# A fused attention and channel-mix kernel: weights in a layout by groups, one store per tile, the last tile in halves, and a searched order

## The chip, the cores and the metric

The kernel runs on one core of a Trainium2 chip. The metric is the time of one execution on the device in microseconds (us); less is better. Engine names are those of the profile: PE is TensorE, DVE is VectorE, ACT is ScalarE, POOL is GpSimd, SP is SyncE, which issues the stores. Labels such as L691 are line numbers of the kernel; the same line can have another number in another run's kernel.

## The reference, cut to what matters

```python
q_s = softmax(q, axis=-1); k_s = softmax(k, axis=2)          # 8 batches, 8 heads, 576 x 64
x = q_s @ (k_s^T @ v)                                        # -> 8 x 576 x 512
xk = mu_k * x + (1 - mu_k) * x_prev                          # x_prev: the token before
xr = mu_r * x + (1 - mu_r) * x_prev
out = sigmoid(xr @ w_r) * (relu(xk @ w_k) ** 2 @ w_v)        # w_k 512x1024, w_v 1024x512, w_r 512x512
```

The output is 4608 rows of 512 float32, 9.44 MB.

## The kernel before

The kernel describes its operations with guessed durations, a small list scheduler in it puts them in an order, and each engine's instructions are emitted in that order. Each batch makes its attention in two groups of four heads (`g` = 0, 1). Each group fills two of the four channel tiles of `xk` and `xr`. The channel mix then works on units of 512 tokens.

Group `g` owns the channel tiles `g` and `g + 2`, and wk comes in one load per group:

```python
    def emit_wk(g):
        ap = bass.AP(tensor=moe_w_k.tensor, offset=moe_w_k.offset + g * 128 * F,
                     ap=[[F, 128], [256 * F, 2], [1, F]])
        ld = nc.gpsimd.dma_start(out=wk_bf[:, g::2, :], in_=ap)
    ...                                             # (cut)
            for cts in ((0, 2), (1, 3)) if early else (range(CT),):
                # matmuls of group 0's two tiles first, then group 1's (cut)
                nc.tensor.matmul(bank(kf)[:, 0:n], lhsT=wk_bf[:, ct, fc::FT],
                                 rhs=xs[0][:, ct, c0:c0 + n], ...)
```

A tile of the output is 128 tokens. They are two pieces of 64 rows in memory, because a column holds position `64 j + r` for row `r * 9 + j`: the rows of one piece are 9 rows apart. It is stored with one DMA for each piece:

```python
            def gated(...):   # DVE: ot = (tanh + 1) * v, 128 x 512
            def store(ot=ot, c=c, half=half):
                for i in range(2):
                    jb = (RING * half + c) // 64 + i
                    bb, j = jb // J, jb % J
                    dst = bass.AP(tensor=out.tensor, offset=out.offset + (bb * S + j) * C,
                                  ap=[[J * C, 64], [1, C]])
                    nc.sync.dma_start(out=dst, in_=ots[ot.index][64 * i:64 * i + 64, :])
```

There are three `ot` buffers in turn, so the fourth tile's gate cannot write before the first tile's store has landed.

The softmax here doesn't subtract the row's maximum and nothing guards it: scores larger than these inputs give would overflow.

## Time and profile before

| | before |
|---|---|
| time, median of 3 runs (range) | 206.43 us (205.68 to 206.51) |
| span of the profiled run | 203.8 us |
| granted PE clock | 1.00 |
| first L691 matmul; second | 16.72 us; 19.17 us |
| last gate starts; span ends | 199.24 us; 203.8 us |
| DMAs of the stores | 72 of 128 KB |

Three lines of the page of before: the span; the busy time of each engine with its share of the span and its instructions; and a count of the DMA packets. A packet under 512 bytes is too short for the data of a store (a row is 2 KB).

```profile
span 203.8 us, 5315 instructions
...
PE 187.2 (92%) x2163; PEld 103.0 (51%) x2163; DVE 162.7 (80%) x348; ACT 135.0 (66%) x211; POOL 39.6 (19%) x63
...
DMA packets 15040, 40.72 MB, mean 200 GB/s; under 512 B 2204, under 2 KB 2728, under 8 KB 15016
```

The windows view of before: in each stretch, its length, then the busy time and count of each engine, the granted clock, the DMA share and GB/s.

```profile
17.40:19.15 1.75, 0.00 (x0) 0.00 (x0) 0.00 (x0) 0.00 (x0) 0.31 (x1) 1.00 1.05 388
...
40.00:60.00 20.00, 19.54 (x343) 10.75 (x341) 19.70 (x36) 19.65 (x29) 8.10 (x12) 1.00 1.04 400
...
120.00:140.00 20.00, 20.00 (x244) 11.16 (x243) 19.24 (x41) 15.65 (x23) 0.00 (x0) 1.00 0.24 55
```

PE is full from 20 us on, except for short waits between 40 and 70 us. But in the first of these stretches, 1.75 us long, no engine computes (POOL's 0.31 us are a load being issued), while the DMA engines run at 388 GB/s. The timeline says what is awaited (the bracket gives the idle time before an instruction and what ended it):

```profile
16.72 0.65 PE L691 MATMUL mm_c<-xk,wk_bf 128*128 128x512 bf16 x1 [0.44 <-DMA wk_bf<-in_moe_w_k_dram]
...
19.17 0.65 PE L691 MATMUL mm_c<-xk,wk_bf 128*128 128x512 bf16 x1 [1.80 <-DMA wk_bf<-in_moe_w_k_dram]
```

The first matmul waits for the first wk load, as it must. The second reads channel tile 2 of the same load, yet waits 1.80 us more, for the second load. Its tile lies between tiles 1 and 3 of that load, whose interleaved pattern covers it: a false overlap.

The tail, from the timeline (x2 counts instructions in the row):

```profile
197.26 1.89 PE L732 MATMUL mm_b<-wv_bf,k_b 128*128 128x512 bf16 x8
...
198.23 1.11 SPq L748 DMA_DIRECT2D out_dram<-ot_b  x2
199.24 0.69 DVE L738 SCALAR_TENSOR_TENSOR ot_c<-th_b,mm_b 128x512 f32<-128x512 f32 x1 [1.04 <-PE mm_b L732]
199.96 1.11 SPq L748 DMA_DIRECT2D out_dram<-ot_c  x2
```

From the start of the last gate to the end of the span there are 203.8 - 199.24 = 4.56 us.

### The profile page before, as it was taken

How to read it: one execution, taken by the hardware profiler on the slowest of the kernel's cores; microseconds unless marked ns; L12 is line 12 of the kernel's file. 1: busy time of each engine (PE TensorE's matmuls, PEld its weight loads, DVE VectorE, ACT ScalarE, POOL GpSimd, SP SyncE). 2: the span in 40 equal slices, each digit the busy share in tenths (PEclk: the TensorE clock that was granted, in tenths of full speed). 3: DMA queues.
4: the chain of work that ended last, by engine and by line, in shares of the span. 5: the costliest groups of instructions: out<-in, count | busy, mean ns of one | idle time of the engine just before them, and what ended most of it. 6: DMA issues, size and time to landing. Idle time of an engine off the chain costs nothing.

```text
span 203.8 us, 5315 instructions
## 1 busy us (share of the span) xinstructions
PE 187.2 (92%) x2163; PEld 103.0 (51%) x2163; DVE 162.7 (80%) x348; ACT 135.0 (66%) x211; POOL 39.6 (19%) x63
## 2 busy tenths in 40 slices
PE   2455999999999999999999999999999999999990
PEld 0241554455644564565467565556556544654840
DVE  2793575799998999999999999999999759832531
ACT  5571696699999896957449788947663643552430
POOL 1682527544353421411100000000000000000000
PEclk9999999999999999999999999999999999999999
DMA  6999999999999999994582220332025122403504
GB/s 211 378 227 329 251 256 401 388 401 406 391 405 393 411 400 398 343 337 171 154 233 53 55 53 3 69 90 51 3 63 119 28 51 55 103 0 69 121 20 103
DMA packets 15040, 40.72 MB, mean 200 GB/s; under 512 B 2204, under 2 KB 2728, under 8 KB 15016
## 3 DMA queue, kind: packets, MB, share of 16 engines
q0 software_dynamic: 7504, 27.40, 39.5%
q1 hardware_dynamic: 7224, 12.40, 21.6%
q10 hardware_dynamic: 288, 0.59, 0.9%
q8 instruction: 17, 0.28, 0.6%
q14 instruction: 7, 0.06, 0.1%
HBM read 33.56 MB, written 9.44 MB: 211 GB/s over the span
## 4 chain that ended last, share of the span: by engine, by line
PE 72%; DVE 10%; DMA 8%; ACT 5%; issue 2%; POOL 0%; SPq 0%; DVEq 0%; ACTq 0%
PE mm_b L691 8%; PE mm_a L732 8%; PE mm_c L691 7%; PE mm_d L691 7%; PE mm_c L732 6%; PE mm_a L691 6%; PE mm_d L732 6%; PE mm_b L732 6%; PE mm_d L722 4%; DMA wk_bf<-in_moe_w_k_dram 4%; PE mm_c L722 4%; DMA raw_d<-in_q_dram 3%; PE mm_a L722 3%; PE mm_b L722 2%; PE att_b L497 2%
## 5 line engine op out<-in xcount | busy, mean ns | idle before, releaser
L691 PEld LDWEIGHTS <-wk_bf 128*128 128x128 bf16 x320 | 43.1, 145 | 24.2 <-DMA wk_bf<-in_moe_w_k_dram 3.2
L691 PE MATMUL mm_b<-xk,wk_bf 128*128 128x512 bf16 (+1 forms) x100 | 24.1, 357 | 0.5 <-DVE xk L553 0.3
L722 PEld LDWEIGHTS <-xr 128*128 128x128 bf16 x144 | 14.0, 98 | 16.3 <-issue 0.2
L732 PEld LDWEIGHTS <-k_b 128*128 128x128 bf16 x144 | 13.7, 98 | 15.8 <-issue 0.2
L732 PEld LDWEIGHTS <-k_a 128*128 128x128 bf16 x144 | 13.5, 98 | 15.3
L691 PE MATMUL mm_d<-xk,wk_bf 128*128 128x512 bf16 (+1 forms) x80 | 20.8, 372 | 0.0
L691 PE MATMUL mm_c<-xk,wk_bf 128*128 128x512 bf16 (+1 forms) x72 | 17.9, 364 | 2.2 <-DMA wk_bf<-in_moe_w_k_dram 2.2
L691 PE MATMUL mm_a<-xk,wk_bf 128*128 128x512 bf16 (+1 forms) x68 | 17.4, 369 | 0.0
L732 PE MATMUL mm_a<-wv_bf,k_a 128*128 128x512 bf16 x48 | 12.3, 380 | 0.0
L732 PE MATMUL mm_c<-wv_bf,k_b 128*128 128x512 bf16 x48 | 12.3, 379 | 0.0
L722 PE MATMUL mm_d<-wr_bf,xr 128*128 128x512 bf16 x44 | 11.3, 379 | 0.0
L732 PE MATMUL mm_d<-wv_bf,k_b 128*128 128x512 bf16 x40 | 10.3, 379 | 0.0
L732 PE MATMUL mm_b<-wv_bf,k_a 128*128 128x512 bf16 x40 | 10.3, 379 | 0.0
L722 PE MATMUL mm_c<-wr_bf,xr 128*128 128x512 bf16 x40 | 10.3, 379 | 0.0
L722 PE MATMUL mm_a<-wr_bf,xr 128*128 128x512 bf16 x36 | 9.3, 379 | 0.0
L676 ACT ACTIVATE rel_c<-mm_b 128x512 bf16<-128x512 f32 (+1 forms) x11 | 6.3, 574 | 4.1 <-PE mm_b L691 4.0
L732 PE MATMUL mm_a<-wv_bf,k_b 128*128 128x512 bf16 x32 | 8.2, 379 | 0.0
L732 PE MATMUL mm_d<-wv_bf,k_a 128*128 128x512 bf16 x32 | 8.2, 379 | 0.0
L727 ACT ACTIVATE th_b<-mm_c 128x512 f32<-128x512 f32 x7 | 4.2, 596 | 5.7 <-PE mm_c L722 4.9
L676 ACT ACTIVATE rel_a<-mm_b 128x512 bf16<-128x512 f32 (+1 forms) x9 | 4.8, 532 | 4.1 <-PE mm_b L691 3.8
L680 DVE TENSOR_TENSOR k_b<-rel_a 128x512 bf16<-128x512 bf16 (+1 forms) x14 | 5.5, 394 | 1.9 <-ACT rel_a L676 1.4
L484 PE MATMUL att_a<-ident,qs_a 64*64 64x64 bf16 x288 | 4.3, 201 | 2.6 <-DVE qs_a L452 2.6
(272 smaller groups left out, 419.6 us busy)
## 6 DMA issues: line engine op xcount, KB each, us to landing
out_dram<-ot_a SPq DMA_DIRECT2D x24, 128.0 KB, 3.0
out_dram<-ot_b SPq DMA_DIRECT2D x24, 128.0 KB, 4.2
out_dram<-ot_c SPq DMA_DIRECT2D x24, 128.0 KB, 2.4
raw_c<-in_v_dram POOLq DMA_DIRECT2D x3, 576.0 KB, 7.7
raw_a<-in_q_dram POOLq DMA_DIRECT2D x2, 576.0 KB, 10.4
raw_b<-in_k_dram POOLq DMA_DIRECT2D x2, 576.0 KB, 9.9
raw_d<-in_q_dram POOLq DMA_DIRECT2D x2, 576.0 KB, 11.1
raw_e<-in_k_dram POOLq DMA_DIRECT2D x2, 576.0 KB, 11.4
```

The source lines that it names most:

```text
L484: nc.tensor.transpose(out=transposed()[64 * u:64 * u + 64, hf, 64 * j:64 * j + 64], in_=qss[qs.index][r, j, 64 * u:64 * u + 64], identity= ...
L497: nc.tensor.matmul(bank(xp)[64 * hf:64 * hf + 64, u, at + c:at + e], lhsT=w[r, hf, :], rhs=qts[qt.index][r, hf, src:src + e - c], start=(n ...
L676: nc.scalar.activation(out=rels[rel.index][:, 0:n], in_=bank(kf)[:, 0:n], func=ACT.Relu, scale=HALF_ROOT)
L680: nc.vector.tensor_tensor(out=k2s[k2.index][:, fc, 0:n], in0=rels[rel.index][:, 0:n], in1=rels[rel.index][:, 0:n], op=ALU.mult)
L691: nc.tensor.matmul(bank(kf)[:, 0:n], lhsT=wk_bf[:, ct, fc::FT], rhs=xs[0][:, ct, c0:c0 + n], start=(ct == 0), stop=(ct == CT - 1))
L722: nc.tensor.matmul(bank(rps), lhsT=xs[1][:, ct, c:c + 128], rhs=wr_bf[:, ct, :], start=(ct == 0), stop=(ct == CT - 1))
L727: nc.scalar.activation(out=ths[th.index][:], in_=bank(rps), func=ACT.Tanh, scale=0.5)
L732: nc.tensor.matmul(bank(vps), lhsT=k2s[k2.index][:, ft, 128 * m:128 * m + 128], rhs=wv_bf[:, ft, :], start=(ft == 0), stop=(ft == FT - 1))
```

## The change

Four intentions: no false overlap on wk; a shorter tail; a better order, found by search; and fewer store issues. The diff, cut to its core (the scheduler's own code was also made faster and got new guesses; that is cut):

```diff
-LOOK = {"PE": 0.03, "ACT": 0.1, "DVE": 0.3, ...}
-AHEAD = (1.0, 4, 2)
+LOOK = {"PE": 0.017, "ACT": 0.686, "DVE": 0.274, ...}
+EARLY = (-0.88, 2.53, 7.27, ...)                 # a lead for each batch and group
+LOADS = ("wk0", "q10b", "wk1", "v10a", "q10a", "wr", "k10a", "wv0", ...)
-WIDE = "DVE"
+WIDE = "ACT"
...
-        ld = nc.gpsimd.dma_start(out=wk_bf[:, g::2, :], in_=ap)
+        ld = nc.gpsimd.dma_start(out=wk_bf[:, 2 * g:2 * g + 2, :], in_=ap)
...                       (xk and xr in the same layout; wr's rows indexed to match)
-            for cts in ((0, 2), (1, 3)) if early else (range(CT),):
+            for cts in ((0, 1), (2, 3)) if early else (range(CT),):
...
+            parts = 2 if half == B // 4 - 1 and c + 128 == RING else 1
+            w = C // parts
...                       (v matmuls, gate and store for each of the parts, e = 0, w, ...)
-            def store(ot=ot, c=c, half=half):
+            def store(e, ot=ot, c=c, half=half, w=w):
+                at = []
                 for i in range(2):
                     jb = (RING * half + c) // 64 + i
-                    bb, j = jb // J, jb % J
-                    dst = bass.AP(tensor=out.tensor, offset=out.offset + (bb * S + j) * C,
-                                  ap=[[J * C, 64], [1, C]])
-                    nc.sync.dma_start(out=dst, in_=ots[ot.index][64 * i:64 * i + 64, :])
+                    at.append((jb // J * S + jb % J) * C)
+                dst = bass.AP(tensor=out.tensor, offset=out.offset + at[0] + e,
+                              ap=[[at[1] - at[0], 2], [J * C, 64], [1, w]])
+                nc.sync.dma_start(out=dst, in_=ots[ot.index][:, e:e + w])
```

So every tile, not only the last, is now stored by one DMA.

## The prediction

> **What bounds it now.** TensorE. In the windows view it is busy without a break from 20.0 to 199.2 us of a 203.8 us span, at clock 1.00. Warm 128x512 matmuls stand 0.216 us apart (groups of four: 0.86 us in the chain of waits). Counted at that step, the matmuls from 20 to 199 us are some 173 us of work in 179 us. The rest is a cold start ([...]pairs take 1.0 us at 20.4 and 22.1 us, 0.43 us from 23.7 us), switches to and from small attention matmuls, and about 1 us of real waiting at 45 to 69 us, where DVE is 96 to 98% busy. So time can be won at the ends: before 20 us and after 199 us.
>
> **Head.** wk comes in two loads. The first L691 matmul starts at 16.72 us, when the first half lands. The second needs channel tile 2, also of the first half, but in the interleaved layout it is ordered behind the second half and starts at 19.17 us; wk_bf's DMA is its releaser in the waits (1.8 us idle). TensorE runs in order, so the attention matmuls of group 1 wait behind it; ACT waits 6.0 us and DVE 3.3 us for them. With contiguous groups, 8 matmuls over the first half (3.4 us cold) and attention pieces fill 17.15 to 19.17 us: 2.0 us. The new order puts 288 KB of q before the second wk half (0.7 us later, about 19.9 us); the filling work lasts past that. The warm-up comes earlier too.
>
> **Tail.** After the last matmul (199.16 us): gate 0.69 us, two store issues of about 0.56 us in a row, transfer; DMA activity ends about 202.5 us, the span at 203.8 us. In halves the last gate is about 0.42 us, one issue goes away, and half the bytes remain while the first half's store ran under the matmuls: 0.9 us. The matmuls keep their sum (128x256 groups of four step 0.44 us). Elsewhere merged stores save SP time that nobody waits for.
>
> **Order.** Total bytes before the last v of batch 1 are the same, so that lands near 37 us as before, and TensorE comes there 2 us earlier. Up to 0.5 us may be lost to this and to DVE, nearly full from 40 to 160 us. Retimed leads, other joins of attention blocks and the mu copy moved from DVE to ACT may give 0.3 to 1.5 us of waits and switches back. Net: 0.4 us gain.
>
> **Sum.** 2.0 + 0.9 + 0.4 = 3.3 us: span 200.5 us, time 206.4 - 3.3 = 203.1 us. Eight in ten: 201.4 to 204.8 us. Chances: faster by over 2% (under 202.3 us) 0.30, within 2% 0.69, slower 0.01.
>
> **What would show it.** Right: the second L691 matmul follows the first at about 17.1 us with no DMA wait; unit 0's last L691 ends near 28.4 us instead of 30.4; the last matmul ends near 196.7 to 197.2 us; from there to the end of the span takes 3.7 us instead of 4.6. Wrong: a wait for the second half of wk after the first eight matmuls, or new waits for xk or DVE between 38 and 50 us.
>
> **What would make it wrong.** Batch 1 too late for a TensorE that is 2 us earlier, so the head gain turns into a wait there (time about 205); or the search finding more than I credit, removing most switches and DVE waits between 36 and 70 us (about 201.5).

## The result, and the profile after

| | before | after |
|---|---|---|
| time, median (range) | 206.47 us (205.68 to 206.53), 4 runs | 277.6 us (276.96 to 279.3), 4 runs |
| span of the profiled run | 203.8 us | 277.5 us |
| mean granted clock | 1.00 | 0.888 |

The ratio is 1.347, with a 95% interval of 1.340 to 1.354. A ratio is the mean time of one kernel's fast runs over that of the other's of the same rounds, so it is not quite the ratio of the medians quoted. The kernel is 71 us slower; the prediction was 3.3 us faster.

The same lines of the page, after, with the line that gives the chain of waits by engine:

```profile
span 277.5 us, 5271 instructions
...
PE 202.1 (73%) x2171; PEld 107.7 (39%) x2171; DVE 161.7 (58%) x348; ACT 137.5 (50%) x212; POOL 40.4 (15%) x65
...
DMA packets 14138, 40.72 MB, mean 147 GB/s; under 512 B 1174, under 2 KB 1954, under 8 KB 14114
...
DMA 58%; PE 21%; DVE 13%; issue 1%; DVEq 0%; SPq 0%; ACT 0%; ACTq 0%
DMA out_dram<-ot_b 23%; DMA out_dram<-ot_c 21%; DMA out_dram<-ot_a 8%; PE mm_c L714 3%; DMA wk_bf<-in_moe_w_k_dram 3%; PE mm_d L714 3%; PE mm_b L714 3%; PE mm_a L714 2%; DMA raw_d<-in_q_dram 2%; PE mm_b L757 2%; DVE ot_c L763 2%; PE mm_c L747 1%; DVE qs_b L468 1%; DVE ot_b L763 1%; DMA raw_a<-in_q_dram 1%
```

DVE, ACT and POOL have the work they had (within 3 us). PE's busy time grew by 15 us, and its granted clock fell to 0.888 in the mean. The traces show the two together: just before a wait of 5.7 us, a group of four 128x512 matmuls takes 0.87 us (from 89.76 us to the next group at 90.63 us); just after it, at 97 to 101 us, the granted clock is 0.50 and a group of four takes 1.7 us. The chain is no longer PE but stores: 52% of the span is spent on three names, `out_dram<-ot_a`, `ot_b` and `ot_c`. PE is at 73%. The waits view of DVE, after, shows how the stores get hold of the compute engines (engine and line, what was waited for, us in total, times, longest):

```profile
DVE ot_b L763 <- DMA out_dram<-ot_b: 21.8, 5, 10.1
DVE ot_c L763 <- DMA out_dram<-ot_c: 20.7, 5, 7.4
DVE ot_a L763 <- DMA out_dram<-ot_a: 19.8, 5, 7.7
```

In before, no wait for a store is among DVE's nine longest; the longest is 3.3 us, for PE. After, gates wait 62 us for the `ot` buffers to come free. DVE's instructions are emitted in one order, and while a gate waits DVE is idle (that is the time in the bracket below), so the squares and the attention behind it wait too. PE then runs out of operands and of `mm` banks (the buffers that its matmuls write). Here an L714 matmul waited 5.70 us for the gate of `ot_b`:

```profile
97.35 1.87 PE L714 MATMUL mm_b<-xk,wk_bf 128*128 128x512 bf16 x4 [5.70 <-DVE ot_b L763]
```

The timeline of DVE shows one of its waits, and the chain puts the store behind it at 32 us:

```profile
73.19 0.69 DVE L763 SCALAR_TENSOR_TENSOR ot_b<-th_a,mm_c 128x512 f32<-128x512 f32 x1 [10.12 <-DMA out_dram<-ot_b]
```

```profile
40.74 32.32 DMA out_dram<-ot_b
```

The number that gives the cause away is in the DMA view of 225 to 260 us, after the loads are done (queue, kind: packets, MB, share of 16 engines):

```profile
DMA packets 889, 1.82 MB, mean 52 GB/s; under 512 B 12, under 2 KB 12, under 8 KB 887
...
q1 hardware_dynamic: 887, 1.79, 13.1%
```

The stores move 52 GB/s without a pause, at 13.1% of 16 engines. Two engines of 16 are 12.5% (the shares of this view run a little high: 1.04 in before, with all 16 busy). In before, stores come in bursts of up to 217 GB/s, in slices of 1 us, with gaps between.

The head did improve in this trace too: the first pair of L714 matmuls runs without a break (two from 17.76 us in 1.07 us, in the chain). That gain is drowned.

### The profile page after: what moved, and what is told of

Same layout as the page of the kernel before. It is cut to its first block, busy times and chain, and to the rows that moved or that the text cites. A ratio compares the mean times of both kernels' runs of the same rounds, so it can differ in the third digit from the quotient of the medians.

```text
span 277.5 us, 5271 instructions
## 1 busy us (share of the span) xinstructions
PE 202.1 (73%) x2171; PEld 107.7 (39%) x2171; DVE 161.7 (58%) x348; ACT 137.5 (50%) x212; POOL 40.4 (15%) x65
## 2 busy tenths in 40 slices
DMA packets 14138, 40.72 MB, mean 147 GB/s; under 512 B 1174, under 2 KB 1954, under 8 KB 14114
## 3 DMA queue, kind: packets, MB, share of 16 engines
HBM read 33.56 MB, written 9.44 MB: 155 GB/s over the span
## 4 chain that ended last, share of the span: by engine, by line
DMA 58%; PE 21%; DVE 13%; issue 1%; DVEq 0%; SPq 0%; ACT 0%; ACTq 0%
DMA out_dram<-ot_b 23%; DMA out_dram<-ot_c 21%; DMA out_dram<-ot_a 8%; PE mm_c L714 3%; DMA wk_bf<-in_moe_w_k_dram 3%; PE mm_d L714 3%; PE mm_b L714 3%; PE mm_a L714 2%; DMA raw_d<-in_q_dram 2%; PE mm_b L757 2%; DVE ot_c L763 2%; PE mm_c L747 1%; DVE qs_b L468 1%; DVE ot_b L763 1%; DMA raw_a<-in_q_dram 1%
## 5 line engine op out<-in xcount | busy, mean ns | idle before, releaser
L714 PEld LDWEIGHTS <-wk_bf 128*128 128x128 bf16 x320 | 45.9, 148 | 60.8 <-issue 42.4
L714 PE MATMUL mm_c<-xk,wk_bf 128*128 128x512 bf16 (+1 forms) x84 | 23.8, 402 | 17.4 <-DVE ot_a L763 7.9
L714 PE MATMUL mm_b<-xk,wk_bf 128*128 128x512 bf16 (+1 forms) x76 | 21.7, 406 | 13.7 <-DVE ot_b L763 8.1
L714 PE MATMUL mm_d<-xk,wk_bf 128*128 128x512 bf16 (+1 forms) x96 | 26.4, 394 | 0.9 <-DVE ot_a L763 0.9
L714 PE MATMUL mm_a<-xk,wk_bf 128*128 128x512 bf16 (+1 forms) x64 | 17.3, 395 | 0.5 <-DVE ot_c L763 0.5
L757 PE MATMUL mm_b<-wv_bf,k_b 128*128 128x512 bf16 (+1 forms) x56 | 13.5, 364 | 1.7 <-DVE ot_c L763 1.7
L699 ACT ACTIVATE rel_c<-mm_c 128x512 bf16<-128x512 f32 (+1 forms) x8 | 4.6, 572 | 15.0 <-PE mm_c L714 8.7
L757 PE MATMUL mm_c<-wv_bf,k_a 128*128 128x512 bf16 x40 | 10.3, 380 | 0.0
L699 ACT ACTIVATE rel_a<-mm_d 128x512 bf16<-128x512 f32 (+1 forms) x9 | 5.2, 576 | 9.5 <-DVE k_b L703 8.4
L699 ACT ACTIVATE rel_b<-mm_b 128x512 bf16<-128x512 f32 (+1 forms) x8 | 4.4, 545 | 9.3 <-PE mm_b L714 8.6
L699 ACT ACTIVATE rel_b<-mm_c 128x512 bf16<-128x512 f32 (+1 forms) x7 | 4.0, 567 | 9.7 <-DVE k_a L703 5.1
L757 PE MATMUL mm_a<-wv_bf,k_a 128*128 128x512 bf16 x32 | 8.3, 380 | 0.0
## 6 DMA issues: line engine op xcount, KB each, us to landing
raw_d<-in_q_dram POOLq DMA_DIRECT2D x2, 576.0 KB, 12.5
```

Of the source, the lines that this page charges most:

```text
L699: nc.scalar.activation(out=rels[rel.index][:, 0:n], in_=bank(kf)[:, 0:n], func=ACT.Relu, scale=HALF_ROOT)
L757: nc.tensor.matmul(bank(vps)[:, 0:w], lhsT=k2s[k2.index][:, ft, 128 * m:128 * m + 128], rhs=wv_bf[:, ft, e:e + w], start=(ft == 0), stop=( ...
```

## The experiments

### First question: is it the stores, the order, or the form of the DMA?

Theory 1: the one store of a tile runs on 2 of 16 DMA engines (after has 13.1% of 16 in the view above) because its target's slowest dimension has size 2; then the divisors of that size matter, which the cuts into 62 + 2, 48 + 16 and 57 + 7 rows below test. Theory 2: the searched order makes the waits. Theory 3: one large DMA with three dimensions is slow by its size or form.

**after_two_stores**: the changed kernel, with the stores given back as two.

```diff
+                for i in range(2):
+                    jb = (RING * half + c) // 64 + i
+                    at = (jb // J * S + jb % J) * C
+                    dst = bass.AP(tensor=out.tensor, offset=out.offset + at + e,
+                                  ap=[[J * C, 64], [1, w]])
+                    nc.sync.dma_start(out=dst, in_=ots[ot.index][64 * i:64 * i + 64, e:e + w])
-                dst = ... ap=[[at[1] - at[0], 2], [J * C, 64], [1, w]]   (one DMA)
```

> The changed kernel, each store given again as two DMAs of 64 rows (the halves of the last tile too). Theory 1, engines: the one store of 128 rows, written as 2 x 64 x w, runs on 2 of 16 DMA engines, and that alone costs the 71 us; then this takes 201.4 to 204.8 us, as predicted for the change, with stores landing in 2 to 7 us as before. Theory 2, order: the searched order makes the waits; then this stays over 260 us.

Measured: 204.88 us (204.26 to 205.25), ratio to before 0.992 (0.9885 to 0.9956). The 71 us are gone with the order kept, so theory 2 falls as their cause. The rest is a gain of only 0.8%, a little outside the expected range; that is the second question.

**before_one_store**: the kernel before, with the one store of the change and nothing else.

```diff
-                    dst = ... ap=[[J * C, 64], [1, C]]                       (two DMAs)
+                dst = bass.AP(tensor=out.tensor, offset=out.offset + at[0],
+                              ap=[[at[1] - at[0], 2], [J * C, 64], [1, C]])
+                nc.sync.dma_start(out=dst, in_=ots[ot.index][:])
```

> The kernel before with one thing changed: one DMA of 128 rows per tile, written as 2 x 64 x 512. Theory 1, engines: about 51 GB/s for stores whenever nothing else moves, each engine share 2/16 = 0.125, 9.44 MB then need 184 us from about 38 us on, more while loads share the engines: 250 to 290 us. Theory 2, order: 206 to 207 us.

Measured: 274.43 us (274.21 to 274.66), ratio 1.329 (1.323 to 1.336). The one edit costs 68 us by itself.

**before_rows_62_2** and **before_rows_48_16**: the kernel before, each 64-row store cut into two plain two-dimensional DMAs. 62 has the divisor 2 and none from 3 to 16; 48 and 16 divide by 16.

```diff
-                    dst = ... ap=[[J * C, 64], [1, C]]
+                    for a, z in ((0, 62), (62, 64)):        # or (0, 48), (48, 64)
+                        dst = ... + J * a rows, ap=[[J * C, z - a], [1, C]]
+                        nc.sync.dma_start(out=dst, in_=ots[ot.index][64 * i + a:64 * i + z, :])
```

> The kernel before with each 64-row store cut in 62 + 2 rows, plain two-dimensional patterns, small DMAs. Theory 1[...]: 62 gives 2 and 2 gives 2, so the stores run on 2 engines again: 250 to 290 us, DMA share 0.125 late. Theory 3, that one large DMA of three dimensions is slow by its size or form: these are small and plain, so 207 to 209 us (two more issues at the end).

Measured: 275.84 us (275.02 to 276.8), ratio 1.336 (1.330 to 1.342).

> The control of the cut: 48 + 16 rows, four DMAs per tile as in 62 + 2, but 48 and 16 both divide by 16. Theory 1: all 16 engines, 207 to 208.5 us (about 1.1 us more than before for two more issues of 0.56 us after the last gate). If cutting into four DMAs itself is what costs, it is as slow as 62 + 2.

Measured: 207.05 us (205.88 to 207.44), ratio 1.002 (0.997 to 1.006).

Theory 3 falls: small plain DMAs are as slow as the large one when their row count is 62 + 2 (275.84 us against 274.43), and as fast as before when it is 48 + 16 (207.05 us against 206.44). What decides between these runs is the slowest size of the pattern (here the number of rows), not the bytes, the dimensions or the number of DMAs.

**before_rows_57_7**: a dose between. 57 is 3 x 19, and 7 is 7.

> A middle dose: the kernel before with each 64-row store cut in 57 + 7 rows. By theory 1 these run on 3 and 7 engines[...]. In sum over the run that is 2.95 MB of stores at 25.7 MB per ms and engine (51.4 GB/s over 2), 115 us, and 78 us for its 16th of the loads: 193 us, less than the span, so the time falls between: 207 to 225 us, far from 275. If anything under 16 engines costs the whole 68 us, it stays near 275.

Measured: 237.38 us (237.19 to 240.01), ratio 1.153 (1.147 to 1.158). It is between, as theory 1 says and the rival does not, but above the expected range: a miss in size. The windows view of this run says where the time went:

```profile
60.00:80.00 20.00, 10.47 (x89) 3.97 (x90) 8.06 (x16) 8.30 (x11) 4.33 (x6) 0.74 0.77 282
...
200.00:220.00 20.00, 20.00 (x101) 11.30 (x99) 10.45 (x24) 7.82 (x14) 0.00 (x0) 1.00 0.20 55
```

From 140 us on PE is full (20.00 of 20 in each slice up to 220), so stores in 57 + 7 rows keep up once the loads are over. The loss falls between 60 and 140 us: there, in slices of 20 us, PE is busy 10.47, 17.14, 13.84 and 18.01 us, and all of DVE's waits for stores (26.8 us) lie there. In most of this stretch loads still run. My estimate summed the work of an engine over the whole run; it was not made for the stretch in which loads and stores meet, and that this is why it missed is argued and not shown. Its 2.95 MB of stores are 40 of a tile's 128 rows, put on one engine; that was an assumption, and no view here shows it. How the engines share their time was not measured.

**The engines counted.** The packets give an independent count. In the packed trace of before, from 20 us on, the queue of the stores (q1) has 4608 packets of 2048 bytes, one for each row of the output, and 1152 packets of 4 bytes: 16 for each of its 72 stores of 64 rows. In after, with 37 stores (35 whole tiles and two halves), there are 74 packets of 4 bytes: 2 for each. So the number of small packets went from 16 to 2 for a store where the stores' share of 16 engines became 13.1%. These are the packet lines of before_one_store, before_rows_62_2, before_rows_57_7 and before_rows_48_16, in four fences:

```profile
DMA packets 13960, 40.72 MB, mean 149 GB/s; under 512 B 1124, under 2 KB 1648, under 8 KB 13936
```

```profile
DMA packets 14176, 40.72 MB, mean 149 GB/s; under 512 B 1340, under 2 KB 1864, under 8 KB 14152
```

```profile
DMA packets 14608, 40.72 MB, mean 171 GB/s; under 512 B 1772, under 2 KB 2296, under 8 KB 14584
```

```profile
DMA packets 16192, 40.73 MB, mean 198 GB/s; under 512 B 3356, under 2 KB 3880, under 8 KB 16168
```

Take one small packet for each engine that a store uses: that is my reading, and the 16, the 2 and the 13.1% above agree with it. Of the 2204 small packets of before, 1152 are those of the stores, so 2204 - 1152 = 1052 belong to other things. Then theory 1 asks for:

| kernel | stores x engines | 1052 + small packets | counted |
|---|---|---|---|
| before_one_store | 36 x 2 | 1124 | 1124 |
| before_rows_62_2 | 72 x (2 + 2) | 1340 | 1340 |
| before_rows_57_7 | 72 x (3 + 7) | 1772 | 1772 |
| before_rows_48_16 | 72 x (16 + 16) | 3356 | 3356 |

All four agree to the packet. The sums 2 + 2, 3 + 7 and 16 + 16 are what was counted; how each splits between its two stores is theory 1's, and other sizes were not run. The changed kernel agrees too: its loads differ a little, so its base is taken from after_two_stores_whole (2252 small packets, 2252 - 72 x 16 = 1100), and 1100 + 37 x 2 = 1174, the count on its page. A second look that needs no count of small packets: in the packed trace of after, from 225 to 255 us, exactly two packets of the stores are in flight for 90% of the time and three for the rest; in before, from 199 to 203.8 us, 16 are in flight for 29% of the time.

**The size of the loss**, an estimate from these traces. Two engines move 51 to 52 GB/s (after, 221 to 260 us), so the 9.44 MB of stores keep both busy for 9.44 / 0.0514 = 184 us. Each engine also carries, if the rest is spread evenly, a sixteenth of everything else: (40.72 - 9.44) / 16 = 1.96 MB, which at the 400 GB/s of all 16 (before, 40 to 60 us; 25 GB/s each) is 78 us. That is 262 us of work for these two engines, and the spans are 272.4 us (before_one_store) and 277.5 us (after). The bound had moved from PE to two DMA engines. In the kernel before, an engine has 9.44 / 16 / 0.025 = 24 us for the stores. The 3 us by which after exceeds before_one_store, although its head is better, are not explained.

### Second question: what are the other parts worth?

**before_layout**: the kernel before with the layout by groups alone. The order of PE's and DVE's instructions is the same.

```diff
-        ld = nc.gpsimd.dma_start(out=wk_bf[:, g::2, :], in_=ap)
+        ld = nc.gpsimd.dma_start(out=wk_bf[:, 2 * g:2 * g + 2, :], in_=ap)
-            ... xs[m][:, g::2, ...]            -   cts in ((0, 2), (1, 3))
+            ... xs[m][:, 2 * g:2 * g + 2, ...] +   cts in ((0, 1), (2, 3))
-                                     rhs=wr_bf[:, ct, :]
+                                     rhs=wr_bf[:, ct // 2 + 2 * (ct % 2), :]
```

> The kernel before with the layout by groups alone (wk, xk, xr, and wr's rows indexed to match); the order of the instructions on each engine is that of before. If the head term of the prediction is right and nothing gives it back: 2.0 us less, 204.4 us, second L691 matmul about 0.43 us after the first. Rival: TensorE comes to batch 1 earlier and waits there for data that comes no earlier; then the unit-0 matmuls end about 2 us earlier and the time is 205.5 to 206.5 us.

Measured: 203.79 us (202.85 to 204.62), ratio 0.987 (0.984 to 0.991), against 206.25 us for before on that chip. A second time, as the base of the last four runs:

> The layout by groups alone, once more, as the base of the three kernels beside it on the same chip: 203.5 to 204.2 us, ratio to before about 0.987.

Measured: 203.66 us (203.14 to 204.12), ratio 0.988 (0.985 to 0.991), against 206.13 us. In the timeline of before_layout the two matmuls are now one pair:

```profile
16.78 1.07 PE L691 MATMUL mm_c<-xk,wk_bf 128*128 128x512 bf16 x2
17.78 0.69 PE L497 MATMUL att_b<-qt_b,wp_c 64*64 64x288 bf16 x8
18.41 1.07 PE L691 MATMUL mm_d<-xk,wk_bf 128*128 128x512 bf16 x2
```

The pieces of group 1 (L497) follow at once; in before they began at 19.75 us. The gain of 2.5 us is kept to the end, and the rival (PE would wait for batch 1 instead) is refuted: the last gate of before_layout starts at 197.16 us, 2.1 us earlier in these two traces.

**after_two_stores_whole**: layout and searched order, without the halves (`parts = 1`, two stores).

> The changed kernel with two stores per tile and the last tile whole again. By the tail term of the prediction the halves are worth 0.9 us, so this would be 205.8 us against 204.9. By the trace of after_two_stores, where four store issues of about 0.6 us stand in a row after the two half gates and the tail is 5.1 us instead of 4.6, the halves with two stores each cost: then this is about 0.4 us faster, 204.4 us.

Measured: 204.41 us (203.72 to 204.69), ratio 0.989 (0.986 to 0.992), in the same rounds as before_layout's 0.987. The halves with two stores each did not help (204.88 us on the other chip). And no gain of the searched order over the layout is seen: 0.6 us more in the medians, with intervals that overlap. Whether it costs is open: the first wk load landed 5.9 us (after_two_queues) to 7.9 us (after) after its issue, so single traces cannot settle half a microsecond in the head.

**layout_halves**: the tail term alone, on the layout by groups: halves, two stores each, all on SP.

```diff
+            parts = 2 if half == B // 4 - 1 and c + 128 == RING else 1
+            # v matmuls, gate and two 64-row stores for each column half of the last tile
```

> The layout by groups, and the last tile in two column halves, two stores of 64 rows for each half, all on SP: the tail term by itself. The prediction valued it at 0.9 us less than the layout alone (with one issue a half). With four issues in a row I expect 0.3 to 0.6 us more than the layout alone.

Measured: 204.59 us (203.82 to 205.26), ratio 0.992 (0.989 to 0.995), which is 0.9 us more than layout_again beside it in the medians; the intervals (0.985 to 0.991 there) overlap a little, but the traces agree with it. Its timeline:

```profile
195.57 0.60 PE L736 MATMUL mm_d<-wv_bf,k_b 128*128 128x256 bf16 x4
...
196.00 0.60 PE L736 MATMUL mm_b<-wv_bf,k_b 128*128 128x256 bf16 x4
196.26 0.42 DVE L742 SCALAR_TENSOR_TENSOR ot_c<-th_b,mm_d 128x256 f32<-128x256 f32 x1 [0.62 <-PE mm_d L736]
196.64 0.42 DVE L742 SCALAR_TENSOR_TENSOR ot_c<-th_b,mm_b 128x256 f32<-128x256 f32 x1
196.87 2.46 SPq L753 DMA_DIRECT2D out_dram<-ot_c  x4
```

The gate is shorter (0.42 us), as predicted. But the scheduler mixes the matmuls of the two halves, so the first half is ready only 0.4 us before the second, and four issues of 0.6 us stand in a row. From the start of the last gate to the end of the span it is 202.0 - 196.64 = 5.4 us, against 4.56 us in before and 4.55 us in layout_again.

**after_two_queues**: after_two_stores, with the second 64 rows of each half of the last tile issued from ACT.

```diff
-                    nc.sync.dma_start(out=dst, ...)
+                    (nc.scalar if parts == 2 and i == 1 else nc.sync).dma_start(out=dst, ...)
```

> The changed kernel with two stores per tile, but those of the last tile's halves issued on two queues, the second 64 rows from ACT. If the issues in a row are what lengthens the tail, two of the four leave it: about 1.1 us less than after_two_stores, 203.7 us. If the transfers or the receipt set the tail, 204.5 to 205.

Measured: 203.42 us (203.22 to 204.91), ratio 0.986 (0.983 to 0.990); in the trace 201.6 - 197.69 = 3.9 us from the last gate to the end. Beside after_two_stores_whole, in the same rounds, it is 1.0 us less in the medians (203.42 against 204.41) and 0.7 us shorter in the tail (4.6 us there); but the intervals overlap (0.986 to 0.992 there), so a gain is suggested and not shown.

**layout_two_queues** (the layout, last tile whole, its two stores on SP and ACT) and **layout_halves_two_queues** (the layout, halves, each half's eight matmuls in one piece so that the first is ready 0.9 us before the second, and the second 64 rows of each half issued from ACT):

> The layout by groups, the last tile whole, its two stores on two queues (SP and ACT). If the second issue of about 0.56 us stands in the tail: 0.4 to 0.6 us less than the layout alone. If receipt and end work set it: the same.

Measured: 203.69 us (203.25 to 204.27), ratio 0.988 (0.985 to 0.991): the same as the layout alone.

> The layout by groups, the last tile in halves, the first half's eight matmuls all before the second's, each half's two stores on two queues. Sum of the parts: the last gate 0.27 us shorter, one issue of 0.56 us and half the last transfer out of the tail: 0.9 to 1.1 us less than the layout alone, about 202.8 us, ratio 0.982 to before. This is the candidate to beat both kernels.

Measured: 203.53 us (202.9 to 203.98), ratio 0.987 (0.984 to 0.990): 0.1 us from the layout alone, within the noise, and its tail is 202.2 - 197.83 = 4.4 us. So the expected 0.9 to 1.1 us is a miss here. In layout_two_queues the issue of 0.56 us did leave, but the tail shrank by 0.25 us only (4.30 us from 4.55 us, one trace each). The likely reason, not tested, is that the first store's transfer had run while the second was being issued.

No version tried is clearly better than the layout alone. That one beats both kernels: against before by 1.2% and 1.3% in two batches, with both intervals below 1.

## Why the prediction was wrong

- **The stores: the step that failed.** The prediction said "Elsewhere merged stores save SP time that nobody waits for" and "one issue goes away", and priced the one DMA as the two that it replaced. Its term for these stores was zero; before_one_store shows 68 us. I costed the issue and the bytes, and not on how many engines the bytes move: 2 of 16, at 52 GB/s, where the prediction took a store to move as before. The new slowest dimension stood in the diff.
- **What would make it wrong.** The prediction named late batch-1 data and a better search. Neither was it: with two stores per tile the same order gives 204.88 us.
- **The head: right.** Predicted 2.0 us, measured 2.5 us in each of two batches, with the mechanism seen in the timeline. PE did not wait for wk's second half. The prediction's cold start and its earlier end are in the timelines: pairs of 128x512 matmuls take 1.0 us at 20.4 us in before and at 16.8 us in before_layout, and stand 0.43 us apart from 23.5 us in before and from 20.5 us in before_layout.
- **The tail: not won, and not tested as it was predicted.** Predicted a gain of 0.9 us with one issue per half. That form exists only with the slow stores: in after the last half gate starts at 261.11 us and the span ends at 277.5 us. With two stores per half the halves are 0.9 us slower in the medians (layout_halves); with two queues they differ by 0.1 us from the layout alone, and by 1.0 us, with overlapping intervals, in the searched order. The gate was sized right (0.42 us). "One issue goes away" rested on the same merged stores that failed.
- **The order: not shown.** Predicted a net gain of 0.4 us; after_two_stores_whole is 0.6 us behind the layout alone, with overlapping intervals.
- **The limits outside the stores** (PE full from 20 us, time at the ends) were read in a way that fits the runs: with the stores repaired, the time is 203.4 to 204.9 us, at or near the predicted range of 201.4 to 204.8 us. Only the head's 2.0 us of the sum is shown by the runs; that the total still comes close is in part luck.

## What to carry to other kernels

Before merging DMAs, look at the slowest dimension of the new target. The sizes 64 and 48 + 16 kept the time here (206.44 and 207.05 us); the size 2 gave up 14 of 16 engines and cost 68 us (274.43 us), 62 + 2 rows cost as much (275.84 us), and 57 + 7 less (237.38 us). If the size cannot be kept, keep the DMAs apart: fewer issues gained little here (twice as many, in before_rows_48_16, cost 0.6 us in the medians, within the noise). When a profile's chain turns into DMAs, divide their share by a sixteenth: the flat 13.1% here was two engines. And cost a crowded engine for the stretch where loads and stores meet as well, not only in the mean of the run: in before_rows_57_7 the loss lay there.
